# Attention and squared-ReLU FFN on one core: turning k and q of a head in one PSUM bank, and a shifted order of the first batch

## Chip, core and metric

The kernel runs on one core of a Trainium2 chip, in one launch. The metric is the device time of that launch in microseconds (us). The core has five engines that work in parallel, each through its own instructions in the order of the program: TensorE (PE in the profile; its weight loads are the row PEld), VectorE (DVE), ScalarE (ACT), GpSimd (POOL) and SyncE (SP), which here issues every DMA. They wait for each other through semaphores.

## The reference

Attention with normalized keys and queries, then an FFN with a squared ReLU. q, k, v and the scales g are float32; w_in and w_out are float64; the output is float32.

```python
# q, k, v: (8 batches, 12 heads, 448 positions, 64)
rmsnorm = lambda x, g: x / np.sqrt(np.mean(x * x, -1, keepdims=True) + 1e-6) * g
scores  = (1 / np.sqrt(64)) * rmsnorm(q, g_q) @ rmsnorm(k, g_k).transpose(0, 1, 3, 2)
scores -= scores.max(-1, keepdims=True)
attn = np.exp(scores); attn /= attn.sum(-1, keepdims=True) + 1e-9
x = (attn @ v).transpose(0, 2, 1, 3).reshape(3584, 768)
h = x @ w_in                       # 768 x 2048
out = (s * np.maximum(h, 0) ** 2 + b) @ w_out
```

## The kernel before

**Precision.** Most products are made of float32 numbers split in two parts, a high part (rounded to the type fp32r) and a low part (the difference): three products hi·hi, hi·lo and lo·hi stand for one. For the scores the two parts lie one under the other in a tile: `ka` holds k_hi in partitions 0 to 63 and k_lo in 64 to 127; `qa` holds q_hi twice; one matmul over 128 partitions gives q_hi·k_hi + q_hi·k_lo. `qb` holds q_lo in its lower half and, in partition 64, the negative row maxima; `kb` holds k_hi and ones. So `qa·ka + qb·kb` is the shifted score.

**Slots.** The 96 heads are taken as 48 pairs `p` of two heads `j`; six pairs make a batch. Attention runs in 384 slots, eight per pair: slot `8p + 4j + c` handles chunk `c` of 112 or 128 keys. A slot of the main loop (L914) emits, in this order: the two matmuls of the transposed score of that slot (`score_t`, L451 and L454); two FFN matmuls as filler; the split and the exponent of a chunk (ScalarE, L466 or L470); the next step of every job that was begun earlier; the jobs listed for the slot; the score of a chunk `AHEAD` slots ahead (L410), whose row maximum VectorE takes (`maximum`, L421), two more FFN matmuls; the late jobs (`convert`, `convert_out`, `invert`); the product with v two slots behind (`weigh`, L513); two more FFN matmuls. The filler of batch b starts eight slots after that batch's last own slot, that is in slot 56 for batch 0: six FFN matmuls a slot, 18 for each of 16 blocks `ffn_in` (L208), blocks 0 and 1 and blocks 14 and 15 interleaved. Slots before 0 (from -22 on) hold only jobs and scores.

**Jobs.** `at(slot, f, ...)` puts a job into a slot; the engines execute in the order of emission, so this list is the order of every queue. A job that yields goes on at the top of the next slot, ahead of that slot's own jobs. With `s0 = 8p` and `s1 = s0 + 4j`:

- pairs 0 to 8 (`NR = 9`): k and q come as rows. `load_rows` (L255, s1-28, at the earliest slot -22 + j), `norm_rows` (L261 on ScalarE, L266 on VectorE a slot later, L269 to L271 on GpSimd another slot later; s1-21), `turn` (L278, s1-14: four transposes of 112 x 64 for k into one bank, four for q into another), `split_turned` (L286 to L293, s1-13 and the two slots after it).
- pairs 9 on: `load` (L248, s0-32), `norm` (L348, L353, L356, L357; s0-28), `keep`, `load_kq`, `spread`, `scale` (L373, L374), `split_kq` (L391 to L395).
- all pairs: `double_kb` (copies k_hi into `kb` by a transfer, s1-10), `shift` (moves the maxima into `qb` by a transfer, s1-6), `take` and `gather` (output and its sums), `invert` (L536, L537; s0+13), `divide` (store of the inverted sums L542 at s0+14, their broadcast L546 at s0+16, the product L555 on GpSimd at s0+18), `split_x` (L562, L563): six a batch, from two slots before the next filler on.

**Weights.** w_in and w_out arrive as float64 words and are converted on the chip. w_in has 24 pieces, four quarters of the FFN's width by six chunks of x. `PACE` lists the slots where one conversion starts; its five steps lie in five slots: two VectorE instructions and a ScalarE one (L135, L138, L136), one (L140), one (L143), the high part on ScalarE (L149), the low part on GpSimd (L151). A piece is read by the FFN blocks of its quarter. `OUT` does the same for w_out's 32 pieces, which are read after slot 384.

**PSUM.** Eight banks are given out in the order in which they were freed (`psum`, `free`).

After slot 384 the second FFN product runs as Strassen's seven products of blocks (`multiply`, L848), which no line of the change touches.

Of the kernel before, what the change touches and what calls it, by code (L numbers as in the profile page):

```python
# [9 lines left out]
F32 = mybir.dt.float32  # L10
F32R = mybir.dt.float32r
I32 = mybir.dt.int32
AF = mybir.ActivationFunctionType
ALU = mybir.AluOpType
# [10 lines left out]

LAST = 15

AHEAD = 10

FIRST = -22  # L30

FILL = (2, 2, 2)

PACE = (-15, -10, *range(1, 61, 5), *range(59, 89, 3))

GAP = 2

STEPS = {0: 2, 1: 3, 2: 4, 3: 5, 5: 6, 6: 7, 8: 8, 9: 9, 11: 10, 12: 11, 13: 12}

OUT = (92, *range(110, 141, 6), *(48 * b + i for b in range(3, 8) for i in range(14, 43, 7)))  # L40


@with_exitstack
def attention_then_relu2_ffn(
# [30 lines left out]
    V, S, G, T = nc.vector, nc.scalar, nc.gpsimd, nc.tensor  # L75

    NPAIR, P, _, SEQ = kq.shape
# [3 lines left out]
    B = NT // SEQ  # L81
    D = P // 2
    NP = NPAIR // B
# [4 lines left out]
    NR = rows0.shape[0]  # L88
    NQ = 4
    QC = SEQ // NQ  # L90
# [15 lines left out]
    free = [f"bank{i}" for i in range(8)]  # L106

    ident = cpool.tile([P, P], F32, name="ident")
# [10 lines left out]
    def psum(name):  # L119

        bank = free.pop(0)
        return ps.tile([P, 512], F32, tag=bank, name=name), bank
# [118 lines left out]
    ap = early.enter_context(tc.tile_pool(name="apool", bufs=1))  # L241
    if True:
        raws, kqs, invs, vrs, nmxs, shs, tks = ({} for _ in range(7))
# [7 lines left out]

        def load_rows(p, j):
            tag = f"{('kq', 'rb')[p % 2]}{j}"
            raw = raws[p, j] = ap.tile([QC, 2, NQ, D], F32, tag=tag, name=f"rows{p}_{j}")
            nc.sync.dma_start(raw, rows0[p, :, j])  # L255

        def norm_rows(p, j):
            raw = raws[p, j].rearrange("p t c d -> p (t c) d")
            n = 2 * NQ
            sq = lp.tile([QC, n, D], F32, tag="al", bufs=2, name=f"sq{p}_{j}")  # L260
            S.activation(  # L261
                sq.rearrange("p i d -> p (i d)"), raw.rearrange("p i d -> p (i d)"), AF.Square
            )
            yield
            ssq = ap.tile([QC, n], F32, tag="ssq", bufs=2, name=f"ssq{p}_{j}")
            V.tensor_reduce(out=ssq, in_=sq, op=ALU.add, axis=AX.X)  # L266
            yield
            ri = ap.tile([QC, n], F32, tag="ri", bufs=2, name=f"ri{p}_{j}")
            G.tensor_scalar(ri, ssq, 1.0 / D, 1e-6, ALU.mult, ALU.add)  # L269
            G.tensor_tensor(ri, ri, mhalf[:QC, :n], ALU.pow)  # L270
            G.tensor_tensor(raw, raw, ri.unsqueeze(2).broadcast_to([QC, n, D]), ALU.mult)  # L271

        def turn(p, j):
            raw = raws.pop((p, j))
            for t in range(2):
                tk, bank = psum(f"tk{p}_{j}_{t}")
                for c in range(NQ):
                    T.transpose(  # L278
                        tk[:D, c * QC : (c + 1) * QC], raw[:, t, c], ident[:QC, :QC]
                    )  # L280
                tks[p, j, t] = tk[:D, :SEQ], bank

        def split_turned(p, j):
            n, a = p % 2, slice(j * SEQ, (j + 1) * SEQ)
            (k, k_bank), (q, q_bank) = (tks.pop((p, j, t)) for t in range(2))
            S.copy(ka[n][:D, a], k)  # L286
            S.activation(qa[n][:D, a], q, AF.Copy, scale=gqk[:D])
            yield
            S.activation(qa[n][D:, a], q, AF.Copy, scale=gqk[:D])
            V.tensor_tensor(ka[n][D:, a], k, ka[n][:D, a].bitcast(F32), ALU.subtract)  # L290
            free.append(k_bank)
            yield
            V.scalar_tensor_tensor(  # L293
                qb[n][:D, a], q, gqk[:D], qa[n][:D, a].bitcast(F32), ALU.mult, ALU.subtract
            )
            free.append(q_bank)

        def load_kq(p, j):
            t = kqs[p, j] = ap.tile([P, 2, SEQ], F32, tag=f"kq{j}", name=f"kq{p}_{j}")
# [79 lines left out]
        qa = [ap.tile([P, 2 * SEQ], F32R, name=f"qa{n}") for n in range(2)]  # L379
        kb = [ap.tile([P, 2 * SEQ], F32R, name=f"kb{n}") for n in range(2)]  # L380
        qb = [ap.tile([P, 2 * SEQ], F32R, name=f"qb{n}") for n in range(2)]
# [15 lines left out]
        def move(to, of):  # L397
            nc.sync.dma_start(to.bitcast(F32), of.bitcast(F32))
# [181 lines left out]
        def end(b):  # L580


            return W * NP * b + (START if b < B else LAST)
# [68 lines left out]
        def at(s_, f, *a):  # L652
            jobs[s_].append((f, a))

        for p in range(NPAIR):
            s0 = W * p
            if p >= NR:
                at(s0 - 32, load, p)
                at(s0 - 28, norm, p)
                at(s0 - 24, keep, p)  # L660
            for j in range(2):
                s1 = s0 + 4 * j
                if p >= NR:
                    at(s1 - 19, load_kq, p, j)
                    at(s1 - 19, spread, p, j)
                    at(s1 - 15, scale, p, j)
                    at(s1 - 13, split_kq, p, j)
                else:
                    at(max(s1 - 28, FIRST + j), load_rows, p, j)
                    at(s1 - 21, norm_rows, p, j)  # L670
                    at(s1 - 14, turn, p, j)
                    at(s1 - 13, split_turned, p, j)
                at(s1 - 10, double_kb, p, j)
                at(s1 - 6, shift, p, j)
                at(s1 + 6, take, p, j)
                at(s1 + 7, gather, p, j)
            at(s0 - (9 if p >= NV else 5), load_v, p)
            if p >= NV:
                at(s0 - 3, split_v, p)
            elif p >= NV3:  # L680
                at(s0 + 3, split_v_rest, p)
            at(s0 + 13, invert, p)
            at(s0 + 14, divide, p, 1)
            at(s0 + 16, divide, p, 2)
            at(s0 + 18, divide, p, 3)
        for b in range(B):
            for g in range(NP):
                at(end(b + 1) - (2 if b < B - 1 else 4) + g, split_x, b, g)
        for s_ in (FIRST, FIRST + 3):
            at(s_, load_piece)  # L690
        for s_ in PACE:
            for n in range(5):
                at(s_ + n, convert, n)
            at(s_ + 3, load_piece)

        for s_ in OUT:
            at(s_ - 5, load_out)
# [92 lines left out]
        raws, g9s, ghs = {}, {}, {}  # L790
# [113 lines left out]
        def within(i):  # L904
            return 0 <= i < NSLOT
# [3 lines left out]
        gqk = cpool.tile([P, 1], F32, name="gqk")  # L909
        sb_s = cpool.tile([P, 1], F32, name="sb_s")  # L910
        sb_b = cpool.tile([P, 1], F32, name="sb_b")
        with tc.manual_schedule(engines=ORDERED):
            begun = []
            for s_ in range(FIRST, NSLOT + LAST + 2):  # L914
# [25 lines left out]
                for f, a in jobs[s_]:  # L940
                    if f in late:
                        continue
                    g = f(*a)
                    if g is not None and next(g, 0) is None:
                        begun.append(g)
                ahead = s_ + AHEAD
                scored = within(ahead)
# [26 lines left out]
            for n in range(NFC - 2):  # L974
# [4 lines left out]
                if n in STEPS:  # L979
                    k = STEPS[n]  # L980
# [24 lines left out]
            for x in range(ROUNDS):  # L1005
                g_load(x + 5)
                g_sums(x + 3)
                p, m = divmod(x, NM)
# [60 lines left out]
```

## Time and profile before

| what | value |
|---|---|
| median of 3 runs | 1400.15 us (1399.1 to 1400.77) |
| the profiled execution | 1402.48 us |
| its span, first to last instruction | 1400.7 us |
| mean granted TensorE clock | 0.996 |
| TensorE, VectorE, GpSimd, ScalarE busy | 98%, 74%, 73%, 62% of the span |
| exponent of slot 0, of slot 56, of slot 60 | 25.20, 122.85, 135.28 us |
| slots 61 to 63 | 2.57 us each |

The profile is of one execution; its span leaves out 1.8 us around it. Times in the trace count from the span's start. "busy" is the time in which an engine has an instruction under way; the ends of matmuls are modelled, so a busy TensorE can be a waiting one. "L293" is line 293 of the kernel. A row of the timeline gives start, duration, engine, line, operation, output<-inputs and count; in square brackets the idle time of the engine before it and what ended it. A row of a group gives the shape, the count, then busy us and mean ns, then idle us before them by releaser.

### The profile page before, as it was taken

The numbers are of one execution on the slowest core, as the hardware profiler recorded it, in microseconds if no ns is written. First come the engines' busy times: TensorE is split into PE (matmuls) and PEld (weight loads), VectorE is DVE, ScalarE is ACT, GpSimd is POOL, SyncE is SP. The second block draws the span as 40 slices with busy tenths as digits, with TensorE's granted clock in tenths as the row PEclk, the third lists the DMA queues.
The fourth block names the chain that finished last, engine by engine and source line by source line (L and its number), as shares of the span: only waits on it lengthen the run. The fifth ranks groups of instructions, "written<-read, shape, count | busy, mean of one in ns | idle before, by whom it ended". The sixth has DMA issues, their size and how long they took to land. (4 is left out here: it accounts for less than half of the span.)

```text
span 1400.7 us, 22180 instructions
## 1 busy us (share of the span) xinstructions
PE 1379.6 (98%) x6976; PEld 1262.0 (90%) x6976; DVE 1038.5 (74%) x1603; ACT 868.8 (62%) x1658; POOL 1021.7 (73%) x940
## 2 busy tenths in 40 slices
PE   7999999999999999999999999999999999999998
PEld 5666888999999899999989989989999999999998
DVE  8999786888888778788788778565766665666655
ACT  5776666777777776776777777654544444444443
POOL 7687788777877787777787776267767777577763
PEclk8999999999999999999999999999999999999999
DMA  5566886777677677677677766354434333233331
GB/s 148 133 174 175 258 242 192 220 239 226 190 238 217 200 235 218 189 228 239 198 219 214 225 188 204 94 160 150 118 91 121 99 99 98 84 120 98 98 97 62
DMA packets 209253, 237.95 MB, mean 170 GB/s; under 512 B 72848, under 2 KB 187024, under 8 KB 209136
## 3 DMA queue, kind: packets, MB, share of 16 engines
q1 hardware_dynamic: 209136, 236.54, 57.6%
q8 instruction: 55, 0.90, 0.3%
q14 instruction: 62, 0.51, 0.1%
HBM read 178.00 MB, written 47.11 MB: 161 GB/s over the span
## 5 line engine op out<-in xcount | busy, mean ns | idle before, releaser
L208 PE MATMUL ph<-x,wih 128*128 128x448 f32 x1536 | 491.7, 366 | 0.5 <-DVE x L563 0.5
L848 PE MATMUL m<-t,gh 128*128 128x384 f32 x1568 | 399.3, 335 | 0.2
L208 PEld LDWEIGHTS ph<-x,wih 128*128 128x128 f32 x1536 | 288.6, 188 | 30.8 <-issue 6.7
L421 DVE TENSOR_REDUCE nmx<-sh 112x1 fp32r<-112x448 f32 x384 | 236.6, 618 | 85.3 <-PE sh L410 82.5
L208 PE MATMUL ph<-x,wil 128*128 128x448 f32 x768 | 294.0, 383 | 0.0
L848 PEld LDWEIGHTS m<-t,gh 128*128 128x128 f32 x1568 | 283.4, 188 | 1.0 <-DVE ot L863 0.9
L470 ACT ACTIVATE st<-st 128x448 f32<-128x448 f32 (+1 forms) x294 | 154.2, 524 | 192.9 <-PE st L454 189.9
L848 PE MATMUL m<-t,gl 128*128 128x384 f32 x784 | 262.6, 335 | 0.3 <-DVE gl L830 0.3
L829 ACT CAST gh<-g 128x896 fp32r<-128x896 f32 x112 | 105.4, 942 | 178.2 <-POOL g L819 178.2
L830 DVE TENSOR_TENSOR gl<-g,gh 128x896 fp32r<-128x896 f32 x112 | 127.7, 1141 | 107.2 <-ACT gh L829 107.2
L815 POOL TENSOR_TENSOR g<-g 128x256 f32<-128x256 f32 x112 | 94.6, 845 | 113.5 <-DVE g L814 113.5
L513 PE MATMUL av<-ah,vs 128*128 128x448 f32 x576 | 164.9, 367 | 0.8 <-DVE al L491 0.5
L451 PE MATMUL st<-qa,ka 128*128 128x448 f32 (+1 forms) x384 | 159.1, 414 | 4.1 <-DVE nmx L421 4.0
L208 PEld LDWEIGHTS ph<-x,wil 128*128 128x128 f32 x768 | 144.3, 188 | 17.9 <-issue 6.7
L478 ACT CAST ah<-st 128x448 fp32r<-128x448 f32 (+1 forms) x294 | 156.8, 533 | 1.3
L555 POOL TENSOR_TENSOR u<-uz,zb 64x448 f32<-64x448 f32 x96 | 126.7, 1320 | 42.1 <-DMA zb<-z_d 38.3
L410 PE MATMUL sh<-ka,qa 128*112 128x448 f32 x384 | 145.5, 382 | 3.6 <-DVE ka L290 1.8
L848 PEld LDWEIGHTS m<-t,gl 128*128 128x128 f32 x784 | 147.1, 188 | 0.6 <-DVE gl L830 0.6
L491 DVE TENSOR_TENSOR al<-st,ah 128x448 fp32r<-128x448 f32 x216 | 132.7, 614 | 18.7 <-ACT ah L478 15.8
L454 PE MATMUL st<-qb,kb 128*128 128x448 f32 (+1 forms) x384 | 140.4, 366 | 0.0
L394 POOL TENSOR_TENSOR ka<-kq,ka 64x448 fp32r<-64x448 f32 x78 | 95.5, 1224 | 57.0 <-ACT ka L391 52.3
L819 POOL TENSOR_TENSOR g<-g 128x256 f32<-128x256 f32 x112 | 125.9, 1124 | 0.0
(93 smaller groups left out, 2398.2 us busy)
## 6 DMA issues: line engine op xcount, KB each, us to landing
kq<-in_dram SPq DMA_DIRECT2D x78, 448.0 KB, 4.9
rb<-i_d SPq DMA_DIRECT2D x78, 448.0 KB, 5.9
r_d<-r SPq DMA_DIRECT2D x128, 224.0 KB, 3.1
raw<-in_dram SPq DMA_DIRECT2D x39, 448.0 KB, 5.1
raw<-r_d SPq DMA_DIRECT2D x64, 256.0 KB, 2.8
w64i<-in_dram SPq DMA_DIRECT2D x24, 512.0 KB, 4.7
w64o<-in_dram SPq DMA_DIRECT2D x32, 384.0 KB, 4.6
kb<-ka SPq DMA_DIRECT2D x96, 112.0 KB, 3.3
```

The lines of the kernel that those rows point to most:

```text
L208: T.matmul(ph[:, :SEQ], w[:, cc, f0 : f0 + P], xs[b, cc][:, part, :], start=n == 0, stop=n == 3 * NCC - 1,)
L410: T.matmul(sh[:QC, :SEQ], qa[p % 2][:, a].rearrange("k (p c) -> k c p", c=NQ)[:, c], ka[p % 2][:, a], start=True, stop=True,)
L421: V.tensor_reduce(out=nmxs[p][:, c : c + 1], in_=sh[:QC, :SEQ], op=ALU.max, axis=AX.X, negate=True)
L451: T.matmul(st[:rows, :SEQ], ka[n][:, keys], qa[n][:, q], start=True, stop=False)
L454: T.matmul(st[:rows, :SEQ], kb[n][:, keys], qb[n][:, q], start=False, stop=True,)
L470: S.activation(st[:rows, :SEQ], st[:rows, :SEQ], AF.Exp)
L478: S.copy(ah[:rows], sts[i][0][:rows, :SEQ])
L491: V.tensor_tensor(al, st[:rows, :SEQ], ah[:rows].bitcast(F32), ALU.subtract)
L513: T.matmul(av[:, :SEQ], x, a, start=kc == 0 and m == 0, stop=kc == 3 and m == len(todo) - 1,)
L555: G.tensor_tensor(u[a], uzs.pop((p, j))[a], zb[a], ALU.mult)
L830: V.tensor_tensor(gl, g9[:, 1:8], gh.bitcast(F32), ALU.subtract)
L848: T.matmul(to, g[:, sa], w, start=m == 0 and n == 0, stop=m == NM - 1 and n == 2,)
```

## The change

Five things are altered.

1. **One turn for k and q.** The host lays the rows of k and q of a chunk side by side, so that `turn` makes four transposes of 112 x 128 into one bank: k in partitions 0 to 63, q in 64 to 127. `split_turned` reads q from the upper half, writes q_hi first to the upper half of `qa`, and makes q_lo (L293) from the upper half into the lower half of `qb`.
2. **q_hi doubled by a transfer.** For pairs 1 to 8 the second ScalarE pass (L289) becomes a DMA from the upper to the lower half of `qa`, issued at the top of the slot after the split. Pair 0 keeps the second pass.
3. **Order of the first pairs.** `AHEAD` is 9 instead of 10; `shift` goes to s1-5; `norm_rows` of pairs 2 to 8 goes to s1-23; the first raw rows (pair 9) are loaded at slot 30 instead of 40.
4. **First batch's sums.** For pairs 0 to 5 `invert` and the first two steps of `divide` come one slot later, the third step one slot (pair 5) or two (pairs 0 to 4) later; the sixth `split_x` of batch 0 one slot later (slot 60).
5. **Conversions.** `PACE` has 1, 6, ... 51 and 60, 63, ... 90 instead of 1, 6, ... 56 and 59, 62, ... 86: 24 as before. The first entry of `OUT` is 100 instead of 92.

```diff
-AHEAD = 10
+AHEAD = 9
...
-PACE = (-15, -10, *range(1, 61, 5), *range(59, 89, 3))
+PACE = (-15, -10, *range(1, 56, 5), *range(60, 91, 3))
...
-OUT = (92, *range(110, 141, 6), *(48 * b + i for b in range(3, 8) for i in range(14, 43, 7)))
+OUT = (100, *range(110, 141, 6), *(48 * b + i for b in range(3, 8) for i in range(14, 43, 7)))
...
         def turn(p, j):
             raw = raws.pop((p, j))
-            for t in range(2):
-                tk, bank = psum(f"tk{p}_{j}_{t}")
-                for c in range(NQ):
-                    T.transpose(
-                        tk[:D, c * QC : (c + 1) * QC], raw[:, t, c], ident[:QC, :QC]
-                    )
-                tks[p, j, t] = tk[:D, :SEQ], bank
+            tk, bank = psum(f"tk{p}_{j}")
+            for c in range(NQ):
+                T.transpose(
+                    tk[:, c * QC : (c + 1) * QC],
+                    raw[:, c].rearrange("p t d -> p (t d)"),
+                    ident[:QC, :QC],
+                )
+            tks[p, j] = tk, bank
 
         def split_turned(p, j):
             n, a = p % 2, slice(j * SEQ, (j + 1) * SEQ)
-            (k, k_bank), (q, q_bank) = (tks.pop((p, j, t)) for t in range(2))
+            tk, bank = tks.pop((p, j))
+            k, q = tk[:D, :SEQ], tk[D:, :SEQ]
             S.copy(ka[n][:D, a], k)
-            S.activation(qa[n][:D, a], q, AF.Copy, scale=gqk[:D])
+            S.activation(qa[n][D:, a], q, AF.Copy, scale=gqk[D:])
             yield
-            S.activation(qa[n][D:, a], q, AF.Copy, scale=gqk[:D])
+            if p == 0:
+                S.activation(qa[n][:D, a], q, AF.Copy, scale=gqk[D:])
+            else:
+                move(qa[n][:D, a], qa[n][D:, a])
             V.tensor_tensor(ka[n][D:, a], k, ka[n][:D, a].bitcast(F32), ALU.subtract)
-            free.append(k_bank)
             yield
             V.scalar_tensor_tensor(
-                qb[n][:D, a], q, gqk[:D], qa[n][:D, a].bitcast(F32), ALU.mult, ALU.subtract
-            )
-            free.append(q_bank)
+                qb[n][:D, a], q, gqk[D:], qa[n][D:, a].bitcast(F32), ALU.mult, ALU.subtract
+            )
+            free.append(bank)
...
-                at(s0 - 32, load, p)
+                at(s0 - (42 if p == NR else 32), load, p)
...
-                    at(s1 - 21, norm_rows, p, j)
+                    at(s1 - (21 if p < 2 else 23), norm_rows, p, j)
...
-                at(s1 - 6, shift, p, j)
+                at(s1 - 5, shift, p, j)
...
-            at(s0 + 13, invert, p)
-            at(s0 + 14, divide, p, 1)
-            at(s0 + 16, divide, p, 2)
-            at(s0 + 18, divide, p, 3)
+            first = p < NP
+            at(s0 + 13 + first, invert, p)
+            at(s0 + 14 + first, divide, p, 1)
+            at(s0 + 16 + first, divide, p, 2)
+            at(s0 + 18 + first + (p < NP - 1), divide, p, 3)
...
-                at(end(b + 1) - (2 if b < B - 1 else 4) + g, split_x, b, g)
+                at(end(b + 1) - (2 if b < B - 1 else 4) + g + (b == 0 and g == NP - 1), split_x, b, g)
```

More of the change, by code (lines that the diff above doesn't have):

```diff
@@ L253, in load_rows @@
             tag = f"{('kq', 'rb')[p % 2]}{j}"
-            raw = raws[p, j] = ap.tile([QC, 2, NQ, D], F32, tag=tag, name=f"rows{p}_{j}")
+            raw = raws[p, j] = ap.tile([QC, NQ, 2, D], F32, tag=tag, name=f"rows{p}_{j}")
             nc.sync.dma_start(raw, rows0[p, :, j])
         def norm_rows(p, j):
-            raw = raws[p, j].rearrange("p t c d -> p (t c) d")
+            raw = raws[p, j].rearrange("p c t d -> p (c t) d")
             n = 2 * NQ
@@ L1052 @@
     rows0 = _np.stack([a.reshape(n, 2, 4, s // 4, d)[:9] for a in (k, q)], 2)
-    rows0 = rows0.transpose(0, 4, 1, 2, 3, 5)
+    rows0 = rows0.transpose(0, 4, 1, 3, 2, 5)
     laid = [kq, rows, rows0, vs, g] + [_np.asarray(inputs[x]) for x in _INS]
```

## The prediction

> **What bounds the kernel now.** I read the page first (busy shares), then the busy times by stage, then the waits of VectorE and TensorE, then stretches of the timeline slot by slot.
>
> ```profile
> PE 1379.6 (98%) x6976; PEld 1262.0 (90%) x6976; DVE 1038.5 (74%) x1603; ACT 868.8 (62%) x1658; POOL 1021.7 (73%) x940
> 30.00:123.00 93.00, 88.17 (x374) 61.59 (x373) 85.08 (x150) 73.37 (x145) 68.74 (x76) 1.00 0.58 152
> 135.00:235.00 100.00, 100.00 (x441) 82.46 (x440) 75.48 (x120) 61.60 (x124) 80.41 (x70) 1.00 0.83 239
> ```
>
> The last two rows are stretches in us: length, then busy time of PE, weight load, DVE, ACT and POOL. TensorE's share of 98% hides two regimes. From about 135 us on, when the FFN of the batch before fills the slots, TensorE never rests: what is saved elsewhere is worth nothing there, and any wait of TensorE is lost for good. Before that, in the first batch, there is no filler, and VectorE is the busiest engine by instructions that really run: 85.1 of 93 us. TensorE's 88.2 us contain waiting, since its ends are modelled. VectorE's 7.9 idle us of that stretch are named by its waits:
>
> ```profile
> DVE x L563 <- ACT x L562: 1.5, 1, 1.5
> DVE ssq L353 <- ACT raw L348: 1.5, 1, 1.5
> DVE ssq L266 <- ACT sq L261: 1.3, 3, 0.5
> DVE nmx L421 <- PE sh L410: 0.9, 2, 0.4
> DVE ka L290 <- ACT ka L286: 0.6, 2, 0.3
> DVE qb L293 <- ACT qa L289: 0.6, 2, 0.3
> ```
>
> All but the two long ones are 0.1 to 0.5 us: VectorE arriving a little before ScalarE or TensorE. So the change is worth (a) what it takes from VectorE's path up to slot 60, and (b) minus whatever wait it makes for TensorE afterwards.
>
> **First raw rows sooner.**
>
> ```profile
> 95.80 0.42 SPq L248 DMA_DIRECT2D raw<-in_dram  x1
> 102.31 0.95 ACT L348 ACTIVATE raw<-raw 128x896 f32<-128x896 f32 x1 [1.64 <-DMA raw<-in_dram]
> ```
>
> The load of pair 9 goes out at 95.80, ScalarE waits 1.64 us for it in slot 44 and VectorE then 1.5. Ten slots earlier (slot 30) nothing waits for it, and its tile has no earlier user: **-1.5**. The load moves on SP's queue from behind slot 40's transfers to behind slot 30's, 0.42 us there.
>
> **ScalarE and TensorE lighter.**
>
> ```profile
> L289 ACT ACTIVATE qa<-tk,gqk 64x448 fp32r<-64x448 f32 x13 | 8.2, 627 | 0.3
> 61.90 0.93 PE L278 MATMUL tk<-ident,rows 112*64 112x112 f32 x8
> ```
>
> L289 goes for pairs 1 to 8: nearly all of these 8.2 of ScalarE's 73.4 us. Eight transposes become four of twice the width: between 0.93 (if cost goes with width) and 0.47 us (if with number) a head. Neither engine sets the pace, so both count only through the small waits: 7.9 - 1.5 - 1.5 leaves 4.9 us of idle. I take two thirds, **-3.2** (bounds 0 and -4.9). The wait of 1.5 at x's split stays mostly, since the conversion begun in slot 51 still lies there: **-0.5**.
>
> **First batch's sums later.** The first step of the inversion (L536) is short when undisturbed and long beside GpSimd work:
>
> ```profile
> L536 DVE TENSOR_SCALAR zt<-zt 128x7 f32<-128x7 f32 x6 | 2.5, 416 | 0.0
> 62.83 0.15 DVE L536 TENSOR_SCALAR zt<-zt 128x7 f32<-128x7 f32 x1
> ...
> 104.89 0.87 DVE L536 TENSOR_SCALAR zt<-zt 128x7 f32<-128x7 f32 x1
> ```
>
> Excess 6 x (0.416 - 0.15) = 1.6 us. One slot later, with the row norms two slots earlier, five of six should miss GpSimd's work: **-1.2** (bounds 0 and -1.6). Later sums cost nothing by themselves; x is split from slot 54 on, one piece now in slot 60 instead of 59, and its reader starts in slot 61.
>
> **The residual of q now crosses partition halves.** This is what speaks against the change. L293 used to read and write the lower half; now it reads q, its scale and q_hi in the upper half and writes the lower. L290 already crosses, lower to upper:
>
> ```profile
> 91.85 0.62 DVE L421 TENSOR_REDUCE nmx<-sh 112x1 fp32r<-112x448 f32 x1
> 92.50 0.62 DVE L290 TENSOR_TENSOR ka<-tk,ka 64x448 fp32r<-64x448 f32 x1
> 93.14 0.69 DVE L266 TENSOR_REDUCE ssq<-sq 112x8 f32<-112x512 f32 x1
> ...
> 94.62 0.68 DVE L293 SCALAR_TENSOR_TENSOR qb<-tk,gqk,qa 64x448 fp32r<-64x448 f32 x1 [0.26 <-ACT qa L289]
> 95.23 0.60 DVE L421 TENSOR_REDUCE nmx<-sh 112x1 fp32r<-112x448 f32 x1
> ```
>
> ```profile
> L293 DVE SCALAR_TENSOR_TENSOR qb<-tk,gqk,qa 64x448 fp32r<-64x448 f32 x13 | 8.7, 671 | 0.6 <-ACT qa L289 0.6
> ```
>
> L421 ends at 92.47 and L290 starts at 92.50; it ends at 93.12 and the next starts at 93.14: no overlap on either side. L293 ends at 95.30 but its follower starts at 95.23: 0.07 overlapped. So a crossing instruction loses about 0.1 us on each side, 0.2 together. No row shows a crossing on the input side, so the bounds are 0 and 0.2; nearest is L290, and I take all. Seventeen heads (13 L293 in the stretch 30 to 123, four before it) x 0.2 = **+3.4**.
>
> The Trainium skill (VectorE: DVE Perf Modes, "Two Vector instructions with no wait between them") states it for inputs as well: an instruction whose input or output starts in another 32-partition group than the last one's in that memory starts only when all earlier ones have finished. By it both L293 and its follower are held; were inputs exempt, the sum would be 3.4 us lower, and no run yet shows which.
>
> **Scores nine slots ahead.**
>
> ```profile
> 137.67 0.36 PE L410 MATMUL sh<-ka,qa 128*112 128x448 f32 x1
> 137.88 0.36 PE L208 MATMUL ph<-x,wih 128*128 128x448 f32 x1
> ```
>
> One L421 (0.62 less its overlap, some 0.5 us) fewer is done when the first batch ends; one score matmul, 137.88 - 137.67 = 0.2 us, moves into TensorE's stage: **-0.3**.
>
> **q_hi by a transfer.** It is issued a slot after the split and needed three slots later.
>
> ```profile
> 30.01 0.55 ACT L466 ACTIVATE e<-st 128x448 f32<-128x448 f32 x1 [2.05 <-PE st L454]
> 122.85 0.54 ACT L466 ACTIVATE e<-st 128x448 f32<-128x448 f32 x1
> DMA to landing us min/median/max: 2.2/2.5/5.9
> SPq L542 <- DVE zt L537: 14.8, 6, 3.7
> ...
> 83.61 0.55 SPq L398 DMA_DIRECT2D kb<-ka  x1
> ```
>
> The first two rows are the exponents of slots 3 and 56: 92.8 / 53 = 1.75 us a slot, three slots 5.25. The transfer of k_hi, same size, lands 2.5 us after issue. On SP it queues behind the store of the sums, which waits for VectorE (six waits, mean 2.5, at most 3.7). Mean wait and median landing take 5.0: **0**, just. Each transfer holds SP's queue for 0.55 us; behind it stand row loads, shifts and v's loads, all due slots later. The row norms, two slots sooner, still come five slots after their load, and the shifts, one later, five before their use: 8.8 us, over the longest landing here, 5.9: **0**. The conversions of w_out, eight slots later, lie in TensorE's stage and are read only after the last slot: **0**.
>
> **No conversion beside x's split.**
>
> ```profile
> 131.58 0.47 PE L451 MATMUL st<-qa,ka 128*128 128x448 f32 x1 [1.85 <-DVE nmx L421]
> 135.28 0.52 ACT L466 ACTIVATE e<-st 128x448 f32<-128x448 f32 x1
> 140.08 0.54 ACT L466 ACTIVATE e<-st 128x448 f32<-128x448 f32 x1 [1.27 <-PE st L454]
> 142.65 0.55 ACT L466 ACTIVATE e<-st 128x448 f32<-128x448 f32 x1
> ```
>
> Slots 56 to 59 take 135.28 - 122.85 = 12.4 us; a slot that TensorE fills takes 142.65 - 140.08 = 2.57, four 10.3. The excess is TensorE's wait of 1.85 for VectorE, which there has the splits of x, a scale and the conversion. Without the latter: **-2.1** (bounds 0 and -2.1). The pieces that are now written later fit in TensorE's stage, where VectorE is busy 75 of 100 us.
>
> **The other end of that move.** Eleven conversions now start in slots 60, 63, ... 90 (before: ten in 59 ... 86). The 24th writes its high part in slot 93 and its low part on GpSimd in slot 94. Who reads it: from slot 56 on six FFN matmuls a slot; block 12 is the first of the last quarter and starts with matmul 216, slot 92; its sixth chunk is matmuls 231 to 233, the last three of slot 94, the middle one on the low part. So the margin of four slots is gone. In slot 94 GpSimd has this to do first:
>
> ```profile
> 201.07 2.59 POOL L357 TENSOR_TENSOR ri<-ri,mhalf 128x14 f32<-128x14 f32 x1
> ...
> 212.84 1.29 POOL L151 TENSOR_TENSOR wil<-wai,wih 128x512 fp32r<-128x512 f32 x1
> ...
> 219.62 1.29 POOL L342 TENSOR_TENSOR vs<-vr,vs 128x512 fp32r<-128x512 f32 x1 [1.82 <-ACT vs L341]
> ...
> 222.59 3.30 POOL L357 TENSOR_TENSOR ri<-ri,mhalf 128x14 f32<-128x14 f32 x1
> 220.72 0.55 ACT L466 ACTIVATE e<-st 128x448 f32<-128x448 f32 x1 [1.18 <-PE st L454]
> 221.94 0.71 PE L208 MATMUL ph<-x,wil 128*128 128x448 f32 x1
> ```
>
> 220.72 is slot 94's exponent, 221.94 the matmul in question. L342 of slot 93 waits for ScalarE's copy in that slot, which follows TensorE, so GpSimd can't run ahead; the power L357 starts at 222.59. With its undisturbed 2.59 and the conversion's 1.29 the low part is there at 226.5: **+4.5** of TensorE standing still (5.2 with the power at 3.30; 0 if the order were another). Nothing later absorbs it.
>
> Sum: -1.5 - 3.2 - 0.5 - 1.2 + 3.4 - 0.3 + 0 - 2.1 = -5.4 up to slot 60, +4.5 in slot 94: **-0.9**. The profiled execution took 1402.48 us (span 1400.7, 1.8 around it), so 1401.6 in its terms; it lies 2.3 above the median of 1400.15. Forecast: **1399.3**. A measurement of this kernel can tell about 0.2%, 2.8 us, from no change.
>
> **Rivals.**
>
> - *Crossing halves on the input side costs nothing*: -0.9 - 3.4, 1395.9. For it: no row shows the cost. Against: L290.
> - *The last piece is in time*, GpSimd being further ahead than I read, or the power done elsewhere: -5.4, 1394.8. Against it: L342's wait for ScalarE.
> - *VectorE keeps its small waits*, because they come from its coupling to TensorE's order and not from ScalarE's load: the 3.2 and 0.5 don't come, +2.8, 1403.0. The change would then not do what it says for ScalarE.
> - *Slower: q_hi lands late.* Place: the odd heads, behind the store of the sums. It decides once wait plus landing pass 5.25 us. With the longest wait, 3.7 + 0.55 + 2.5 = 6.7, 1.5 late, six times: +9 - 0.9, 1408.3. Against it: the wait begins before the slot of the transfer, and the mean one is 2.5.
>
> **How the numbers follow.** Forecast 0.55 (its own range 1396.8 to 1402), free crossing 0.12, last piece in time 0.12, small waits kept 0.13, late q_hi 0.08. The predicted time is the forecast's. The range, 1394.5 to 1403.8, takes in the first three rivals and leaves out the late q_hi and the tails. Faster by over 0.2%: 0.10 of the forecast's 0.55 and most of the first two rivals, 0.31; slower: the fourth, half of the third and 0.04, 0.18; the same: 0.51.
>
> **What would show it.** Right: no wait of L348 for its load; L293 starting at its predecessor's end, its follower at its own; L536 near 0.15 in all six; slot 56 some 3 us sooner and slots 56 to 59 at 2.57 each; one wait of TensorE at L208 on GpSimd's L151 of 4 to 5 us near slot 94. Wrong: no such wait, or TensorE's L410 waiting for transfers of qa in the first 120 us.

## The result, and the profile after

| | before | after |
|---|---|---|
| median | 1400.46 us (4 runs, 1399.1 to 1401.5) | 1415.54 us (4 runs, 1413.72 to 1419.19) |
| ratio | 1 | 1.0112 (1.0089 to 1.0134) |
| the profiled execution, its span | 1402.48, 1400.7 us | 1414.79, 1412.7 us |
| granted TensorE clock | 0.996 | 0.989 |
| start of slots 0, 56, 60 | 25.20, 122.85, 135.28 us | 28.81, 129.29, 139.91 us |

The changed kernel is slower by 1.1%. The forecast was 1399.3, the range ended at 1403.8. The list of TensorE's waits says where to look. After (engine, operation, line, then what it waited for: us in total, times, longest):

```profile
PE sh L414 <- DMA qa<-qa: 11.2, 5, 4.6
PE tk L277 <- POOL rows L271: 7.4, 4, 2.9
PE ph L208 <- POOL wil L151: 3.8, 1, 3.8
```

The first row is new, and it is the one that the prediction named as the sign of being wrong: scores (L414) that wait for the transfer of q_hi. The third is the wait that it did foresee. The second existed before (4.7 us, like here all ahead of slot 0). It grew by 2.7 us, but experiments 1 and 3 below have 7.3 and 7.8 us of it and start slot 0 no later than the kernel before, so it isn't the loss.

To see what each is worth, I compare the times at which the exponents of the same slots start. After minus before, in us: slot 0 +3.6, slot 24 +5.6, slot 56 +6.4, slot 60 +4.6, slot 92 +5.4, slot 96 +11.0, slot 108 +11.6, the last instruction +12.0. So the loss has two places: the time before slot 24, and slot 94. In between a little is won and lost, and after slot 108 only 0.4 us are added.

**The first place.** The timeline of TensorE, after: the first score that waits, ahead of slot 0, and the one of slot 23.

```profile
27.32 0.70 PE L414 MATMUL sh<-ka,qa 128*112 128x448 f32 x1 [4.60 <-DMA qa<-qa]
...
68.88 0.70 PE L414 MATMUL sh<-ka,qa 128*112 128x448 f32 x1 [3.85 <-DMA qa<-qa]
```

ScalarE and SyncE's queue ahead of the second one:

```profile
60.14 0.63 ACT L289 ACTIVATE qa<-tk,gqk 64x448 fp32r<-64x448 f32 x1
```

```profile
60.49 0.56 SPq L402 DMA_DIRECT2D qb<-nmx  x1
61.14 1.28 SPq L328 DMA_DIRECT2D vf<-in_dram  x2
62.47 0.62 SPq L130 DMA_DIRECT2D w64i<-in_dram  x1
63.20 0.51 SPq L402 DMA_DIRECT2D qa<-qa  x1
```

q_hi is there at 60.77, but its transfer goes out at 63.20: a shift of maxima, two loads of v and a load of w_in are issued first, in order. It lands 5.5 us later, at 68.7, and TensorE, ready since 68.88 - 3.85 = 65.03, stands still. From the end of the split to the first score there were 4.3 us; 2.4 went in the queue and 5.5 in landing. Over all its transfers, q_hi's landing reads:

```profile
DMA to landing us min/median/max: 2.2/3.5/5.5
```

All five waiting scores are the first ones of even heads (slots -1, 7, 15, 23, 39); before each, the transfer was issued 0.4 to 2.8 us after the split had ended. A shift and two loads of v stand right ahead of it in all five.

The waits cost more than their length, since the granted clock falls. Stretches of before, then of after (length, busy us of PE, PEld, DVE, ACT, POOL, then the clock, DMA share and GB/s):

```profile
14.00:30.00 16.00, 12.06 (x49) 8.34 (x49) 15.40 (x27) 8.86 (x16) 12.12 (x15) 0.75 0.40 110
60.00:90.00 30.00, 29.41 (x132) 21.03 (x130) 28.04 (x51) 24.81 (x50) 23.78 (x27) 1.00 0.61 166
```

```profile
14.00:30.00 16.00, 6.87 (x20) 5.09 (x21) 13.87 (x23) 6.60 (x12) 14.04 (x15) 0.50 0.42 111
60.00:90.00 30.00, 26.05 (x99) 17.92 (x98) 26.50 (x46) 20.11 (x39) 20.82 (x24) 0.94 0.62 159
```

The duration of a score matmul goes with it, as far as its modelled end can tell: 0.70 us at 68.88, where an undisturbed one takes 0.36.

**The second place.** TensorE's matmuls of slot 94 and GpSimd, both after:

```profile
231.68 0.47 PE L208 MATMUL ph<-x,wil 128*128 128x448 f32 x1 [3.82 <-POOL wil L151]
231.98 0.36 PE L208 MATMUL ph<-x,wih 128*128 128x448 f32 x1
...
233.24 0.57 PE L208 MATMUL ph<-x,wil 128*128 128x448 f32 x1
...
236.97 0.37 PE L208 MATMUL ph<-x,wil 128*128 128x448 f32 x1
```

```profile
227.81 2.59 POOL L361 TENSOR_TENSOR ri<-ri,mhalf 128x14 f32<-128x14 f32 x1
230.36 1.26 POOL L151 TENSOR_TENSOR wil<-wai,wih 128x512 fp32r<-128x512 f32 x1
```

The order is the one worked out beforehand: the power, then the low part, then the matmul at once (230.36 + 1.26 = 231.62). But the slot costs 11.03 - 5.41 = 5.6 us, 1.8 more than the wait that is shown: the matmuls behind it run slowly for a while (0.57 us at 233.24, 0.37 again at 236.97). The clock was halved for one stretch of 3.41 us, and before and behind it it was whole:

```profile
232.25:235.66 3.41, 3.41 (x11) 2.57 (x9) 0.84 (x2) 2.31 (x5) 1.36 (x2) 0.50 0.03 10
```

Half of 3.41 is 1.7 us, about what the slot costs beyond the wait.

### The profile page after: what moved, and what is told of

It is laid out like the page before. It is cut to its first block, busy times and chain, and to the rows that moved or that the text cites. A ratio compares the mean times of both kernels' runs of the same rounds, so it can differ in the third digit from the quotient of the medians.

```text
span 1412.7 us, 22065 instructions
## 1 busy us (share of the span) xinstructions
PE 1378.2 (98%) x6904; PEld 1261.5 (89%) x6904; DVE 1038.8 (74%) x1603; ACT 863.9 (61%) x1642; POOL 1016.4 (72%) x940
## 5 line engine op out<-in xcount | busy, mean ns | idle before, releaser
L820 POOL TENSOR_TENSOR g<-g 128x256 f32<-128x256 f32 x112 | 95.0, 849 | 114.5 <-DVE g L819 114.5
L414 PE MATMUL sh<-ka,qa 128*112 128x448 f32 x384 | 147.1, 385 | 15.2 <-DMA qa<-qa 11.2
L414 PEld LDWEIGHTS sh<-ka,qa 128*112 128x112 f32 x384 | 107.8, 281 | 25.2 <-DVE bits L140 7.8
```

The lines of the kernel that those rows point to most:

```text
L414: T.matmul(sh[:QC, :SEQ], qa[p % 2][:, a].rearrange("k (p c) -> k c p", c=NQ)[:, c], ka[p % 2][:, a], start=True, stop=True,)
```

## The experiments

**Theory.** The loss is two waits, each with a clock that falls behind it: the transfer of q_hi stands in SyncE's queue (7 us or so), and slot 94 (5.6). **Rival.** The waits only show where something else is late (the one bank, the residual that crosses halves), and another wait takes their place when they go. The expectations give each theory a letter: A is the first theory, B its rival, and further letters stand for narrower questions that came up on the way. Kernels run side by side share their runs of the kernel before, whose medians were 1401.04 us (experiments 1, 2, 3 and 5), 1400.98 (4, 8, 9 and 10) and 1400.26 (6, 7 and 11). Differences between medians of different groups below are not corrected for this, which can make up to 0.8 us.

**1. ScalarE's second pass for every pair, no transfer.**

```diff
-            if p == 0:
-                S.activation(qa[n][:D, a], q, AF.Copy, scale=gqk[D:])
-            else:
-                move(qa[n][:D, a], qa[n][D:, a])
+            S.activation(qa[n][:D, a], q, AF.Copy, scale=gqk[D:])
```

> The changed kernel with the second pass of q_hi on ScalarE again for all pairs (from the upper half of the bank); all else as changed. Theory A (the transfers land late, TensorE waits 11.2 us for them in five waits and then runs at a lower granted clock for some us): slot 56 comes back by 6 us or more, the startup's 3.6 us too, and the time falls by 6 to 8 us from 1415.5, to 1407.5 to 1409.5. Rival B (VectorE's path, longer by the crossing of halves, is the bound and the waits for the transfers only show where TensorE stands idle anyway): the time falls by less than 2 us and TensorE waits for VectorE or ScalarE instead.

Measured: 1415.67, ratio 1.0102 (1.0087 to 1.0117). Nothing was won, which by itself speaks for the rival. VectorE's waits in this kernel, from 30 to 123 us:

```profile
DVE ka L292 <- ACT qa L291: 8.5, 7, 1.8
```

The five waits for the transfer are gone and slot 0 starts 0.6 us sooner than in the kernel before, but seven times VectorE waits up to 1.8 us with the residual of k (L292) for ScalarE's second pass over q (L291). The two touch different halves, but now one bank; in the kernel before, k and q had a bank each. So this run removed one wait and made another, and didn't separate the theories; that needs a copy which doesn't touch the bank (experiment 4). The wait is one of the program's semaphores. The Trainium skill (PSUM — Partial Sum Buffer, "PSUM bank collisions raise a hardware error") lets two engines use different quarters of a bank's partitions at once, so a finer semaphore might do; no run here tried it.

**2. The conversions of w_in two slots sooner, all else as in the change.**

```diff
-PACE = (-15, -10, *range(1, 56, 5), *range(60, 91, 3))
+PACE = (-15, -10, *range(1, 56, 5), *range(58, 89, 3))
```

> The changed kernel with the late conversions in slots 58, 61, ... 88 instead of 60, 63, ... 90, so that the last low part is written in slot 92; all else as changed. Theory A: the wait of 3.8 us in slot 94 goes together with the lower clock behind it (5.6 us between slots 92 and 96), and up to 1 us comes back beside the split of x: 1410 to 1411. Rival C (the clock behind the wait has another cause than the wait): only the 3.8 us go: 1411.7 to 1412.7.

Measured: 1410.11, ratio 1.0066 (1.0051 to 1.0081), 5.4 less than the change. The wait for L151 is gone; slots 92 to 96 lose nothing (+4.06, +4.01). TensorE's waits:

```profile
PE sh L414 <- DMA qa<-qa: 13.4, 5, 4.7
...
PE av L517 <- DVE al L495: 2.8, 2, 2.2
```

The first shows that the two losses are apart. The second is new: 2.2 us near slot 106, taken up in experiment 7.

**3. The same transfer, issued on ScalarE's queue.**

```diff
-                move(qa[n][:D, a], qa[n][D:, a])
+                S.dma_start(qa[n][:D, a].bitcast(F32), qa[n][D:, a].bitcast(F32))
```

> The changed kernel with the transfer of q_hi issued from ScalarE's queue, right behind the pass that wrote it, instead of SyncE's; all else as changed. If it is late because it queues on SyncE behind waits for VectorE, most of the waits of TensorE go and the time falls by 4 to 7 us, to 1408.5 to 1411.5. If the landing itself (2.2 to 5.5 us) is what is too long, two or three of the five waits stay and the time is 1413 or more. Rival B (VectorE bound): less than 2 us either way.

Measured: 1408.57, ratio 1.0053 (1.0036 to 1.0069), 7.0 less than the change. Slot 60 comes at -3.9 against the kernel before instead of +4.6. ScalarE and its queue:

```profile
31.22 0.63 ACT L289 ACTIVATE qa<-tk,gqk 64x448 fp32r<-64x448 f32 x1
31.87 0.54 ACT L470 ACTIVATE e<-st 128x448 f32<-128x448 f32 x1
31.88 0.47 ACTq L294 DMA_DIRECT2D qa<-qa  x1
```

```profile
DMA to landing us min/median/max: 2.2/3.4/5.3
```

The transfer leaves 0.03 us after the split. It lands as it did before (3.4 against 3.5), so what SyncE's queue cost was the order of issue, not a slower transfer. Two waits of at most 0.8 us are left.

**4. The copy by ScalarE out of SBUF, no transfer.**

```diff
-            if p == 0:
-                S.activation(qa[n][:D, a], q, AF.Copy, scale=gqk[D:])
-            else:
-                move(qa[n][:D, a], qa[n][D:, a])
+            S.copy(qa[n][:D, a], qa[n][D:, a].bitcast(F32))
```

> The changed kernel with the lower half of q_hi copied by ScalarE out of the upper half of qa in SBUF, instead of by a transfer; all else as changed. The run with ScalarE's second pass out of the bank stayed at 1415.7 because VectorE's k_lo waited there 8.7 us for that pass (theory D: k and q now share a bank, and the two engines' reads of it are put in order). Theories A and D: with the copy off the bank both kinds of wait go, slot 56 comes at before's 122.9 or up to 2 us later, and the time is 1406 to 1410. Rival B (VectorE's path with the crossing of halves and ScalarE's extra pass are the bound): slot 56 stays 4 us or more late and the time is 1412 to 1416.

Measured: 1407.09, ratio 1.0047 (1.003 to 1.0064), 8.4 less than the change. VectorE's waits from 30 to 123 us:

```profile
DVE x L564 <- ACT x L563: 1.5, 1, 1.5
DVE ka L292 <- ACT qa L289: 0.8, 2, 0.5
```

The same work on the same engine as in experiment 1, with its source in SBUF and not in the shared bank: the 8.5 us of waits are gone and slot 60 comes at -5.0. So the bank was what experiment 1 paid for, and the late transfer costs the change 7 to 8.4 us.

**5. Both lists of the change in the kernel before, nothing else of it.**

```diff
-PACE = (-15, -10, *range(1, 61, 5), *range(59, 89, 3))
+PACE = (-15, -10, *range(1, 56, 5), *range(60, 91, 3))
-OUT = (92, *range(110, 141, 6), *(48 * b + i for b in range(3, 8) for i in range(14, 43, 7)))
+OUT = (100, *range(110, 141, 6), *(48 * b + i for b in range(3, 8) for i in range(14, 43, 7)))
```

> The kernel before with the conversions' slots of the change alone (both lists). Theory A: the wait in slot 94 appears, 3.8 us and some 1.8 us of lower clock, and slots 56 to 59 win about 2 us: 1400.5 + 5.6 - 1.8 = 1404.3. Rival C (no clock effect): 1400.5 + 3.8 - 2.1 = 1402.2. If the wait in slot 94 needs the other parts of the change: 1398.5.

Measured: 1409.18, ratio 1.0061 (1.0046 to 1.0076), 4.9 above theory A's time. Slots 56 to 60 win 2.4 us (-0.25 to -2.62; the sum had 2.1), slot 94 costs 6.8 (-2.39 to +4.43) where 5.6 were expected, and slots 96 to 108 lose another 2.4 that the expectation doesn't have (experiment 7). The stretches around slot 94:

```profile
220.00:224.00 4.00, 0.17 (x2) 0.12 (x1) 0.00 (x0) 0.00 (x0) 3.82 (x2) 0.88 0.64 197
224.00:230.00 6.00, 6.00 (x15) 4.45 (x16) 1.24 (x2) 2.31 (x5) 3.02 (x3) 0.51 0.22 82
230.00:234.00 4.00, 4.00 (x20) 3.43 (x19) 2.66 (x4) 2.10 (x4) 2.75 (x3) 1.00 0.80 189
```

TensorE stands still for one stretch, and in the next six us its clock is 0.51: 15 matmuls instead of the 28 that the next experiment shows. Then it is whole again. The halved stretch in full:

```profile
223.03:229.86 6.83, 5.98 (x14) 4.44 (x15) 1.24 (x2) 2.31 (x5) 3.68 (x4) 0.50 0.33 126
```

The Trainium skill (TensorE: Matmul & The Clock Gate, "Part 1: The HAM clock gate") has the clock halved after an idle window of about 3.4 us and whole after a busy one of the same length. The halving agrees (3.8 us idle). The slow stretch agrees in the change (3.41 us) and is twice as long here (6.83 us). So the same wait of 3.8 us makes slot 94 cost 5.6 us in the change and in experiment 4, and 6.8 here; what decides between the two lengths was not seen.

**6. The same kernel, with 16 products of the identity ahead of the last FFN matmuls of slot 94**, the first of which waits for GpSimd.

```diff
+                if s_ == 94:
+                    warm_up(16)
```

> The kernel before with the conversions' slots of the change (both lists), and 16 extra products of the identity with itself on TensorE in slot 94, between the last product with v and the matmul that waits for GpSimd; their result is not used. Theory F (the granted clock halves because TensorE stands still for some 4 us, and stays halved for 6 us more): the extra work fills the wait, the clock stays at 1.00, slot 94 costs about 4 us instead of 6.8, and the time is 1406 to 1407 against 1409.2 without them. Rival C (the clock falls for another reason): the clock falls all the same, and the time is 1409 or more.

Measured: 1406.59, ratio 1.0041 (1.0026 to 1.0057), against 1409.18 and 1.0061 (1.0046 to 1.0076) without them. The same stretches:

```profile
220.00:224.00 4.00, 3.75 (x29) 3.37 (x28) 0.00 (x0) 0.09 (x1) 2.68 (x2) 1.00 0.61 191
224.00:230.00 6.00, 6.00 (x28) 5.00 (x27) 3.37 (x6) 4.25 (x9) 4.89 (x4) 1.00 0.37 91
```

The low part comes no sooner, but the clock stays whole and the slot costs 4.0 instead of 6.8 us. These 2.8 us are the price of TensorE having stood still, not of the late piece (2.6 us between the medians).

**7. The list of w_in alone in the kernel before (w_out's conversions stay at slot 92).**

```diff
-PACE = (-15, -10, *range(1, 61, 5), *range(59, 89, 3))
+PACE = (-15, -10, *range(1, 56, 5), *range(60, 91, 3))
```

> The kernel before with the change's list of w_in conversions alone, w_out's first conversion in slot 92 as before. Theory E (the conversion of w_out in slots 100 to 105 beside the split of batch 1's x costs 2.2 us near slot 106): 1407, that is 2 us below the run with both lists (1409.2). Rival: 1409, and the wait near slot 106 is still there.

Measured: 1405.89, ratio 1.0038 (1.0024 to 1.0052), against 1409.18 with both lists. Here slot 94 costs 7.6 us and nothing is lost behind it (+4.06 in slot 96, +4.11 in slot 108, +3.41 at the end); with both lists 2.4 us are lost from slot 96 to 108. VectorE near slot 106 in the kernel with both lists, and what TensorE waits for there:

```profile
253.71 0.55 DVE L170 SCALAR_TENSOR_TENSOR wao<-w64o,wao 128x384 f32<-128x384 f32 x1
254.18 1.57 DVE L374 SCALAR_TENSOR_TENSOR kq<-kq,gqk,rb 128x448 f32<-128x448 f32 x1
255.67 1.56 DVE L563 TENSOR_TENSOR x<-u,x 128x448 fp32r<-128x448 f32 x1
257.15 0.61 DVE L491 TENSOR_TENSOR al<-st,ah 128x448 fp32r<-128x448 f32 x1
257.68 0.61 DVE L421 TENSOR_REDUCE nmx<-sh 112x1 fp32r<-112x448 f32 x1
258.21 0.61 DVE L563 TENSOR_TENSOR x<-u,x 128x448 fp32r<-128x448 f32 x1
```

```profile
PE av L513 <- DVE al L491: 2.2, 1, 2.2
```

A step of w_out's conversion (L170) now stands in VectorE's queue beside a scale (L374) and the split of batch 1's x (L563), both 1.6 us long here, where the undisturbed split in the last row takes 0.6. The low part of the attention weights (L491), which the product with v needs, comes behind them.

The move of w_out's conversion to slot 100 also has a good side. With it at slot 92, as here and in experiment 8, GpSimd's power ahead of the late piece takes 3.30 us and TensorE waits 5.1 us in slot 94 (5.0 in experiment 8); with it at slot 100 the power takes 2.59 and the wait is 3.8:

```profile
219.45 3.30 POOL L357 TENSOR_TENSOR ri<-ri,mhalf 128x14 f32<-128x14 f32 x1
```

**8. The change with w_out's first conversion back at slot 92.**

```diff
-OUT = (100, *range(110, 141, 6), *(48 * b + i for b in range(3, 8) for i in range(14, 43, 7)))
+OUT = (92, *range(110, 141, 6), *(48 * b + i for b in range(3, 8) for i in range(14, 43, 7)))
```

> The changed kernel with the first conversion of w_out in slot 92 again instead of 100; all else as changed. Theory E: in slots 100 to 105 it lies beside the split of batch 1's x and costs TensorE up to 2.2 us of waiting for VectorE near slot 106 (seen in the four runs so far, 0.4 us in the profile of the change): 1413 to 1414. Rival: nothing, 1415.5, the wait comes from other work there.

Measured: 1414.78, ratio 1.01 (1.0085 to 1.0115), 0.8 less than the change, within the scatter of the two. Inconclusive; in the change's own profile the wait near slot 106 is small as well (the slots 96 to 108 lose 0.5 us), and slot 94 costs 6.8 us here. The 2.2 us are there in experiments 1, 2, 3, 5 and 6, and not in the change's profile nor in experiment 4, all seven with the conversion at slot 100; that it depends on where the engines stand when slot 106 comes is likely, but not shown.

**9. The change with three things mended: transfer on ScalarE's queue, w_in's conversions at 58 to 88, w_out's at 92** (the edits of 3, 2 and 8 together).

> The changed kernel with the transfer on ScalarE's queue, the late conversions in slots 58, 61, ... 88, and w_out's first conversion in slot 92. If the three losses (late transfers, slot 94, slot 106) are all that went wrong and add up: 1408.6 - 6.9 - 1.9 = 1399.8, the same as before within noise; slots 56 to 60 ahead of before by 2 to 4 us. If a rival loss is left, 1403 or more.

Measured: 1399.48, ratio 0.9991 (0.9981 to 1.0), 16.1 less than the change. Alone the edits gave 5.4 + 7.0 + 0.8 = 13.2; but experiments 2 and 3 each lose 2.4 us from slot 96 to 108, where the change loses 0.5, and with w_out's conversion back at 92 that is not lost: 1.9 each more, 17.0. The losses add up, to within 1 us. TensorE's one wait for q_hi:

```profile
PE sh L414 <- DMA qa<-qa: 0.8, 1, 0.8
```

What is left of the change is then worth 1.5 us in the median, which is within the noise, 3.8 us at slot 60 and 3.7 at the end of the profile (the profiled execution of the kernel before took 2 us more than its median).

**10. Experiment 9 with the halves exchanged: q in the lower, k in the upper half.**

```diff
-            k, q = tk[:D, :SEQ], tk[D:, :SEQ]
+            q, k = tk[:D, :SEQ], tk[D:, :SEQ]
...
-                qb[n][:D, a], q, gqk[D:], qa[n][D:, a].bitcast(F32), ALU.mult, ALU.subtract
+                qb[n][:D, a], q, gqk[:D], qa[n][:D, a].bitcast(F32), ALU.mult, ALU.subtract
...
-    rows0 = _np.stack([a.reshape(n, 2, 4, s // 4, d)[:9] for a in (k, q)], 2)
+    rows0 = _np.stack([a.reshape(n, 2, 4, s // 4, d)[:9] for a in (q, k)], 2)
```

> As the run with the transfer on ScalarE's queue and both lists of conversions mended, but with q in the lower and k in the upper half of the bank, so that the residual of q (L293 before) stays in the lower half and only the residual of k crosses. If crossing costs VectorE 0.2 us a head and VectorE sets the pace: 2 to 3.4 us less than that run. If the crossing is hidden by other waits: the same within 1 us.

Measured: 1395.58, ratio 0.9964 (0.9951 to 0.9977), 3.9 less than experiment 9, half a microsecond more than expected. VectorE around the residual of q (L297), in the change and then here:

```profile
99.21 0.62 DVE L425 TENSOR_REDUCE nmx<-sh 112x1 fp32r<-112x448 f32 x1
99.87 0.69 DVE L297 SCALAR_TENSOR_TENSOR qb<-tk,gqk,qa 64x448 fp32r<-64x448 f32 x1
100.59 0.63 DVE L425 TENSOR_REDUCE nmx<-sh 112x1 fp32r<-112x448 f32 x1
```

```profile
90.51 0.62 DVE L425 TENSOR_REDUCE nmx<-sh 112x1 fp32r<-112x448 f32 x1
91.06 0.67 DVE L297 SCALAR_TENSOR_TENSOR qb<-tk,gqk,qa 64x448 fp32r<-64x448 f32 x1
91.65 0.61 DVE L425 TENSOR_REDUCE nmx<-sh 112x1 fp32r<-112x448 f32 x1
```

In the change L297 starts 0.04 us after its predecessor's end, and its follower 0.03 after its own. Where q stays in its half, each starts 0.07 to 0.08 before the other's end. The three together take 1.75 us instead of 2.01. So it is in all 18 heads of the change, and here L297 overlaps in 17 of 18. The residual of k crosses in both kernels.

**11. Experiment 10 with the copy by ScalarE out of SBUF.**

```diff
-            if p == 0:
-                S.activation(qa[n][D:, a], q, AF.Copy, scale=gqk[:D])
-            else:
-                S.dma_start(qa[n][D:, a].bitcast(F32), qa[n][:D, a].bitcast(F32))
+            S.copy(qa[n][D:, a], qa[n][:D, a].bitcast(F32))
```

> The run with q in the lower half and both lists of conversions mended, but with the upper half of q_hi copied by ScalarE out of SBUF instead of by a transfer on ScalarE's queue. If ScalarE has room for the copy and the transfer still cost some waits (0.8 us at the start, four of 0.2 to 0.5): 1393.5 to 1395. If ScalarE's load matters: 1396 to 1398.

Measured: 1394.90, ratio 0.996 (0.9945 to 0.9975), the lowest median of all, though not apart from experiment 10. No wait for q_hi is left (experiment 10 had four, of at most 1.0 us). It is faster than the kernel before by 0.4% and than the change by 1.5% (their intervals, 0.9945 to 0.9975 and 1.0089 to 1.0134 of before, are well apart).

## Why the prediction was wrong, step by step

- **"q_hi by a transfer: 0, just."** This step failed. It is 8.5 us at slot 60 (experiment 3 against the change: -3.9 against +4.6), 7.0 and 8.4 in the medians of experiments 3 and 4. I had the queue's worst wait from the store of the sums and took a mean and a median to make 5.0 against 5.25 us, which is no margin for 16 transfers. I had also looked for the wait in the wrong place: the rival *q_hi lands late* had the right mechanism and a fair price (9 us) but put it on the odd heads behind the store of the sums. It was the even heads, behind a shift, the loads of v and, in the case shown, one of w_in; the step had named shifts and v's loads only as what stands behind the transfer, not ahead of it. The landing, too, I took from one median (2.5 us); it was 3.5 and up to 5.5. And the first pairs, whose jobs are crowded together ahead of slot 0, were not looked at: 3.6 us were lost there.
- **Slot 94: "+4.5".** Order, place and wait were right (3.8 us shown), and nothing absorbed it. The term was mis-sized: 5.6 us in the change, 6.8 and 7.6 in experiments 5 and 7, since the halved clock behind it was left out (3.41 us in the change, 6.83 in both experiments). In experiment 7 the wait itself is 5.1, close to the 5.2 that the step gave for the longer power.
- **"Conversions of w_out: 0."** Their reader is late, as the step said; what it left out is VectorE's queue, where a step of theirs lies beside the split of x. It costs 2.4 us in experiment 5 (3.3 between the medians of 5 and 7), but only some 0.5 in the change's own profile, where it also shortens the wait in slot 94 (experiment 7).
- **Crossing: +3.4.** Right, if a little small: 3.9 us between experiments 9 and 10, and no overlap on either side of L297. The Trainium skill (VectorE: DVE Perf Modes, "Two Vector instructions with no wait between them") has inputs held as well, and here they are. The rival *free crossing* falls.
- **First raw rows: -1.5.** Right: VectorE's sum of squares has no wait left (L357, 0.0 in the last column of its group), nor has ScalarE one for the load. Groups of VectorE from 30 to 123 us, after:

```profile
L357 DVE TENSOR_REDUCE ssq<-raw 128x14 f32<-128x896 f32 x1 | 1.1, 1086 | 0.0
L540 DVE TENSOR_SCALAR zt<-zt 128x7 f32<-128x7 f32 x5 | 1.1, 217 | 0.0
```

- **First batch's sums: -1.2.** Right: the five in the second row take 0.217 us on average instead of 0.416, and the sixth, at 126.7, takes 0.16; 1.2 us less in all. It isn't firm: in experiment 10 two of the six are long again (0.85 and 0.58 us).
- **Slots 56 to 59: -2.1.** Right: 139.91 - 129.29 = 10.6 us, before 12.4, predicted 10.3.
- **ScalarE and TensorE lighter: -3.2, x's wait: -0.5.** Too large, and for a reason that doesn't hold. VectorE's idle time from slot 3 to 56 is 7.8 us of 92.8 before and 4.7 of 92.1 both in experiment 3 and in experiment 4; 1.5 of the difference is the raw rows, so the small waits gave 1.6. Experiment 4 has ScalarE's pass back and the same idle time, and experiment 11 gives it back too and loses nothing: ScalarE's load was not what made VectorE wait. Whether the four transposes fewer or the new order did is open. x's wait stayed whole (1.5 us in experiment 4), so its 0.5 didn't come.

So it is partly luck that the total looks right without the late transfer: up to slot 60 the sum was -5.4 and experiment 9 is at -3.8; without the crossing the sum is -8.8 and experiment 10 is at -8.4, where a crossing worth more (4.6 us at slot 60) makes up for small waits worth less. From slot 3 to 56 the kernel before took 92.8 us, the change 96.3, experiment 10 took 88.0.

Sum in the profile's terms: predicted -0.9, measured +12.0, 12.9 apart. Of these 10.0 lie up to slot 60 (8.5 the transfer; the rest small terms), 0.8 from there to slot 92, 1.1 in slot 94, and 1.0 after it.

**Left open.** The medians lie 15.1 us apart, the profiled executions 12.3; runs of the change scatter more (5.5 us) than those of the kernel before (2.4), and which wait varies from run to run was not seen. Where between 2.9 us (experiment 8 at 105 us, the clock stays at 1.00) and 3.8 us (halved) the idle time begins to cost clock, these runs don't tell, nor why the halved stretch lasts 3.4 us in some and 6.8 in others. `AHEAD` and the later shift were not tried alone.

## What to carry to other kernels

Before a pass of an engine is replaced by a transfer, list what is issued ahead of it on its queue in each position of the schedule, the crowded start too, and set the longest queueing plus the longest landing against the time to its reader; if that doesn't fit, another engine's queue may do. Price a wait of TensorE of about 4 us with the slow clock behind it (here another 1.8 to 3.0 us), and look for dummy matmuls only where the wait can't go. When two tiles are put into one bank, ask which engines read its halves in the same slot, and lay the tiles out so that VectorE's instructions stay in the half that their neighbours in its queue use.

## What the runs showed of the hardware

- ScalarE's instructions, too, can stop overlapping where the partition half changes. In the kernel before, the instruction behind the first pass over q starts 0.1 us before that pass ends; the one behind the second pass, which reads the lower half and writes the upper, starts 0.02 us after it ends (87.25 against 86.60 + 0.63). Crossing within one instruction isn't what decides: in the change the pass over q (L289) stays in the upper half, behind a copy of k in the lower, and no neighbour overlaps it in any of the 18 heads. And in experiment 4 the copy that crosses from the upper to the lower half of SBUF starts 0.1 us before its predecessor's end in 9 of 18 heads. The exact rule is not shown. From the change:

```profile
89.68 0.54 ACT L470 ACTIVATE e<-st 128x448 f32<-128x448 f32 x1
90.12 0.51 ACT L288 CAST ka<-tk 64x448 fp32r<-64x448 f32 x1
90.64 0.63 ACT L289 ACTIVATE qa<-tk,gqk 64x448 fp32r<-64x448 f32 x1
91.30 0.54 ACT L470 ACTIVATE e<-st 128x448 f32<-128x448 f32 x1
```

- Standing still for 3.8 us halved TensorE's clock, for 3.41 us in the change and for 6.83 us in experiment 5; 16 products of the identity in the same wait kept it at 1.00 (experiment 6).
- A DMA of 112 KB within SBUF took 2.2 to 5.5 us to land, from SyncE's queue as from ScalarE's (experiment 3).
